# Two attention layers on one core: one quad's exps given to GpSimd as powers of 2, and the sums' copies put ahead of a small load

## The chip, the cores and the metric

The kernel runs on one core of one Trainium2 chip. The metric is the device time of one execution in microseconds (us), as the median of the runs shown; an execution that is profiled has a time of its own, given beside its span. The engines are TensorE (PE, with its weight loads PEld), VectorE (DVE), ScalarE (ACT), GpSimd (POOL) and SyncE (SP, here a DMA queue only).

## The reference, cut to what matters

```
x: [2048, 512]; A: 32 heads of 16, one shared key and value (MQA); B: 32 heads of 16, a key and value each
A: q = x @ wq, k = x @ wk, v = x @ wv
B: q, k, v = x @ wqkv
each: p = softmax(q @ k.T * 16 ** -0.5) over 2048 keys;  o = p @ v;  o @ wo
g = sigmoid((x * gate_w).sum(-1));  out = g * A + (1 - g) * B
```

So there are 64 heads with 2048 x 2048 scores each: 268 million exps. The kernel takes no maximum off before the exp; the row sums come out of the value product through columns of ones beside the values.

## The kernel before

**Work.** The scores are made transposed, keys on the partitions, in units of 128 x 1024 scores (64 keys for each of two blocks of 512 queries, two heads). Two units make a quad (the list `quads`), 32 quads a phase, and 32 phases the kernel: 2048 units in all. Phases go by four: a group is eight heads of layer a or b (the groups alternate a, b), in two halves of the queries and four heads at a time. PE makes a unit's scores (L751) in one of four PSUM tiles, `slot0` to `slot3`; an engine turns them into probabilities in one of 16 SBUF tiles (`prob`, `vec`); PE multiplies these with the values (L836) into the slot that collects the phase, and behind the phase's last quad VectorE copies that slot out (L904). `normalised` then sends the sums to DRAM and back in another layout (`held`, `each`, `back`), takes their reciprocals, and moves the products to where the output product needs them. The output products (`o_unit`), the projections of queries, keys and values (`project`) and their splitting into two f16 halves fill the gaps.

**Who makes the exps.** ScalarE makes most units with one ACTIVATE each (L782). VectorE makes the rest, whole quads taken from a phase's end (`vector_job`, `chain`): for layer a seven instructions a unit, the first from PSUM (L1003), two on the bits in SBUF (L1007, L1011) and four of a polynomial (L1016); for layer b three (L1036, L1039, L1043). Before the change GpSimd makes none: it sets a few tiles and issues DMAs.

**Order.** All of it is written out by a planner in Python while the program is built. It keeps a clock for each engine (`plan.pe`, `plan.act`, `plan.dve`, `plan.pool`, `plan.sp`), adds a fixed cost for each instruction, and at every step lets PE take the next job that the clocks allow:

```
EXP, EXP_ENDS, EXP_AFTER = 916, 1148, 456
ISSUE, ISSUE_SP, LANDS, SUM_LANDS = 480, 600, 3200, 6500
a = plan.vec(convert, 1130, 1, t + TO_VEC, (), spared)
```

What it decides is then fixed: each engine runs its list in that order, waiting by semaphores for what another engine has not finished. A tile that a DMA still reads is given back to the list of free tiles at a planned time (`returns`, `put_back`, `returned`).

Of the kernel before, what the change touches and what calls it, by code (L numbers as in the profile page):

```python
# [12 lines left out]
F32 = mybir.dt.float32  # L13
# [3 lines left out]
ALU = mybir.AluOpType  # L17
# [27 lines left out]

EXP, EXP_ENDS, EXP_AFTER = 916, 1148, 456
SCORES, HALF, PRODUCT = 215, 430, 215
SLACK, TIGHT, URGENT, SOON, AHEAD = 404, 404, 300, 500, 900
BLOCK, READ, SPACED = 256, 3400, 1500
TO_VEC, FROM_VEC, CHAINED = 255, 150, 130  # L50
X_JOB = 560
# [120 lines left out]
def _fast(ctx, tc, x, wq_a, wk_a, wv_a, wo_a, wqkv_b, wo_b, gate_w, out, flag):  # L172
# [98 lines left out]
        return later  # L271

    warm = cst.tile([P, 1], F32, name="warm")
    index = cst.tile([P, P], F16, name="index")
    level = cst.tile([P, P], F16, name="level")
    nc.vector.memset(kA[:, :BLK], 0.0)
# [121 lines left out]
    def hold():  # L398
        pair[1] = min(slots, key=slot_at)
        free["spare"] = busy[id(pair[1])] = math.inf  # L400
# [35 lines left out]
    def starts_in(m):  # L436

        return plan.act + 2 * max(m - at[0], 0) * EXP * 0.93
# [18 lines left out]
    def reads():  # L457

        for m, fn in list(waiting):
            if at[0] >= m and not (half_vec and half_vec[0] // 2 < m):  # L460
                waiting.remove((m, fn))
                fn(plan.pe)

# [166 lines left out]
    def normalised(n, half, q, raw, turned, now):  # L630

        src, gi = groups[n]
        ends = n + 1 == len(groups) and half and q
        o, d = turned[:, 0], turned[:, 1]
        queues = (nc.sync, nc.scalar, nc.gpsimd) if ends else (nc.sync,)
        if src == "a":
            moves = [(part, slice(k, P + k - 1, 2), 0, ROWS) for k, part in ((1, d), (0, o))]
        else:
            moves = [(d, DH, 0, 2), (d, 5 * DH, 2, 2), (o, 0, 0, 1), (o, 3 * DH, 1, 2), (o, 7 * DH, 3, 1)]
            moves = [(part, slice(at, at + n * DH), to * DH, n * DH) for part, at, to, n in moves]  # L640
        moves = [(*move, e) for t in (d, o) for e in range(2) for move in moves if move[0] is t and (ends or t is o)]
        if not ends:
            each = ops.tile([P, 2 * DH], F32, tag="each", name=f"each{n}{half}{q}", bufs=1)
            held, back = (dram.tile([2 * 4, BLK], F32, tag=tag, name=f"{tag}{n}{half}{q}", bufs=2) for tag in ("held", "back"))
            heads = [(slice(1, P, 2 * DH), 4)] if src == "a" else [(slice(DH, P, ROWS), 2), (slice(2 * DH, P, ROWS), 2)]
            to = 0
            for which, count in heads:
                nc.sync.dma_start(held.rearrange("(e h) q -> h e q", e=2)[to : to + count], raw[which])
                to += count
            nc.sync.dma_start(each, held.rearrange("h (c j) -> (h c) j", c=DH))  # L650
        for m, (part, at, to, n_rows, e) in enumerate(moves):
            queues[m % len(queues)].dma_start(part[ROWS * e + to :][:n_rows], raw[at, e])
        plan.sp = max(plan.sp, now) + (len(moves) + 3) * ISSUE_SP
        returns.append((plan.sp + LANDS, raw))
        o16 = ops.tile([P, 2, BLK], F16, tag="o16", name=f"o16{n}{half}{q}", bufs=8)
        o16s[n, half, q] = o16
        cut = P if ends else BLK // 2

        def over(c):
            nc.vector.reciprocal(d[:, c : c + cut], d[:, c : c + cut])  # L660

        def gated():
            nc.vector.reciprocal(each, each)
            nc.vector.scalar_tensor_tensor(each, each, UP, gate_in[:, "ab".index(src), half], op0=ALU.mult, op1=ALU.mult)

        def spread(end):
            def moved():
                nc.sync.dma_start(back.rearrange("h (c j) -> (h c) j", c=DH), each)
                for e in range(2):
                    for h in range(4):  # L670
                        at = h if src == "a" else h % 2 * 2 + h // 2
                        nc.sync.dma_start(d[ROWS * e + h * DH :][:DH], back[4 * e + at : 4 * e + at + 1].to_broadcast([DH, BLK]))

            begun[0] = plan.on_sp([moved], end, 9 * ISSUE_SP) + 2 * LANDS

        def times(c):
            if ends:
                nc.vector.scalar_tensor_tensor(o[:, c : c + cut], o[:, c : c + cut], UP, d[:, c : c + cut], op0=ALU.mult, op1=ALU.mult)
            else:
                nc.vector.tensor_tensor(o[:, c : c + cut], o[:, c : c + cut], d[:, c : c + cut], op=ALU.mult)  # L680

        def high(c):
            (nc.scalar.copy if ends else nc.vector.tensor_copy)(o16[:, 0, c : c + cut], o[:, c : c + cut])  # L683

        def low(c):
            nc.vector.tensor_sub(o16[:, 1, c : c + cut], o[:, c : c + cut], o16[:, 0, c : c + cut])

        if ends:
            tail.append((over, times, high, low))
            return  # L690
        due = now + (30000 if n + 1 < len(groups) else 6000)
        begun = [math.inf]

        def then(end):
            ready["o16", n, half, q] = end + FROM_VEC
            put_back(end + FROM_VEC, turned)

        def spreads(end):
            spread(end)
            for c in range(0, BLK, cut):  # L700
                b = plan.vec(lambda c=c: times(c), 330, 3.4, begun[0], (), None, due)
                e = plan.vec(lambda c=c: high(c), 200, 3.3, 0.0, (b,), None, due)
                plan.vec(lambda c=c: low(c), 330, 3.2, 0.0, (e,), then if c else None, due)

        plan.vec(gated, 430, 3.5, now + 7500, (), spreads, due,
                 room=lambda: ready.get("gates", math.inf) <= plan.dve)
# [5 lines left out]
    probs, pending, vector = {}, {ph: [] for ph in range(len(phases))}, set()  # L712
    free_tiles, owed, returns = deque(tile for tile in prob_tiles if tile is not prob_tiles[-2]), [0], []
    at, part, pv_at, put_in = [0], [0], [0], [0]
    half_vec, chains = [], {}
    wrote = {"n": 0, "seen": 0}
    borrowed = {}
    filled, since = deque(), {}
# [1 line left out]
    def put_back(t, *tiles):  # L720
        for tile in tiles:
            since[id(tile)] = t
            free_tiles.append(tile)

    def spare_tiles():
        return max(len(free_tiles) - owed[0] - len(filled), 0)
# [5 lines left out]
    def laid(ph, c, p):  # L732
        n, half, q = phases[ph]
        src, gi = groups[n]
        t = ready.get(("q", src, gi, half, p), math.inf)
        if src == "b":
            t = max(t, ready.get(("k", "b", gi, c // 8, p), math.inf))
        return t

    def products(u, bank):  # L740
        m, e = divmod(u, 2)
        ph, c, w = quads[m]
        n, half, q = phases[ph]
        src, gi = groups[n]
        p = q + e
        k = kA if src == "a" else K[gi, p]
        for hh in range(2):
            for a in range(0, P, COLS):
                key = c * P + (a + ROWS * w) % P
                j = a // ROWS  # L750
                nc.tensor.matmul(bank[a : a + COLS, hh], k[rows(hh), key : key + COLS],  # L751
                                 Q[src, gi, half, p][rows(hh), j * BLK : (j + 1) * BLK], start=True, stop=True)
# [179 lines left out]
    def pick(now):  # L932
# [15 lines left out]
            return None  # L948
        return 2 * found[-1]

    def pressing():

        if not half_vec:
            return False
        ph = quads[half_vec[0] // 2][0]
        return ph <= quads[min(at[0], len(quads) - 1)][0] and left_in(ph) * EXP < CHAIN
# [116 lines left out]
    def spare_job(now):  # L1073

        if current:
            return current[0].jobs[0]
        if free["spare"] > now or min(slot_at(slot) for slot in slots) > now:
            return None
        if put_in[0] >= QUADS - 2 and put_in[0] + len(pending[pv_at[0]]) >= QUADS:
            return None  # L1080
        if half_vec:
            job = vector_job(now)
            if job or pressing():
                return job
        able = [u for u in units if u.can(now)]
        if not hurry(now):
            job = vector_job(now)
            if job:
                return job
        if not able:  # L1090
            return None
        unit = min(able, key=lambda u: u.due())
        if spare_tiles() < BEGIN and not hurry(now) and len(unit.jobs) > 8 and at[0] < 32 * LASTS:
            return None
        units.remove(unit)
        unit.begin()
        current.append(unit)
        hold()
        return unit.jobs[0]
# [195 lines left out]
    def returned():  # L1295

        for back in list(returns):
            if back[0] <= plan.pe:
                returns.remove(back)
                put_back(back[0], back[1])  # L1300

    def past(m):
        return lambda: at[0] >= m
# [399 lines left out]
```

## Time and profile before

| | |
|---|---|
| two timed runs | 1767.23 and 1771.4 us, median 1769.32 us |
| profiled execution | 1778.6 us, its span 1776.7 us |
| PE busy | 1721.5 us (97%) |
| PEld busy | 994.1 us (56%) |
| VectorE busy | 1310.5 us (74%) |
| ScalarE busy | 1706.3 us (96%), 1840 exps among it |
| GpSimd busy | 192.2 us (11%), nearly all of it DMA issue |

A row of a group names the line, the engine, the operation, the tiles (written <- read), the shapes and the count, then busy us and mean ns. A row of waits names who waited for what: us in all, times, longest. A row of a line's own view gives the shortest, median and longest duration in ns, and when the first and the last began. A row of the timeline gives start and duration in us. Instructions of one engine overlap a little, so durations add up to more than the pace.

### The profile page before, as it was taken

Reading aid. Unit: us, or ns where it says so; the run is one execution under the profiler, and the core shown is the slowest. Engines: PE = TensorE matmul, PEld = TensorE weight load, DVE = VectorE, ACT = ScalarE, POOL = GpSimd, SP = SyncE. Lnnn points to the kernel's source line nnn. Section 1 sums busy time; section 2 is a strip of 40 time slices with the busy share of each in tenths; the row PEclk is TensorE's granted clock in tenths of the full one; section 3 lists DMA queues with packets and bytes.
Section 4 is the critical chain, followed back from the end, with each engine's and each line's share of the span. In section 5 each row is a group of like instructions: output and inputs, shape, how many; then the busy total and the mean of one; then the engine's idle time right before and its main releaser. Section 6 shows DMA issues by size and latency. Waiting matters only on the chain. (4 is left out here: it accounts for less than half of the span.)

```text
span 1776.7 us, 109255 instructions
## 1 busy us (share of the span) xinstructions
PE 1721.5 (97%) x51099; PEld 994.1 (56%) x51099; DVE 1310.5 (74%) x1503; ACT 1706.3 (96%) x1856; POOL 192.2 (11%) x314
## 2 busy tenths in 40 slices
PE   8999999999999999999999999999999999999996
PEld 5555655555555565555655566555555555545453
DVE  5467689986758784996774976699586787499944
ACT  5999999999999999999999999999999999999994
POOL 1101000000000111001111121000211221100000
PEclk9999999999999999999999999999999999999998
DMA  4212110113122222112223222111322322111321
GB/s 144 68 44 61 46 41 22 40 35 72 38 55 52 53 67 61 31 37 51 45 52 64 45 66 54 50 28 40 65 39 53 58 59 70 28 46 29 105 64 63
DMA packets 71152, 95.12 MB, mean 54 GB/s; under 512 B 27580, under 2 KB 36060, under 8 KB 70692
## 3 DMA queue, kind: packets, MB, share of 16 engines
q1 hardware_dynamic: 53892, 58.61, 12.4%
q0 software_dynamic: 13568, 27.22, 7.8%
q8 instruction: 402, 6.59, 1.6%
q10 hardware_dynamic: 3232, 2.23, 0.4%
q14 instruction: 58, 0.48, 0.1%
HBM read 23.45 MB, written 17.81 MB: 23 GB/s over the span
## 5 line engine op out<-in xcount | busy, mean ns | idle before, releaser
L782 ACT ACTIVATE prob<-slot 128x1024 f32<-128x1024 f32 x1121 | 1115.9, 1101 | 15.7 <-PE slot L751 9.1
L782 ACT ACTIVATE vec<-slot 128x1024 f32<-128x1024 f32 x707 | 734.8, 1104 | 11.4 <-PE slot L751 7.5
L836 PE MATMUL slot<-prob,vA 64*32 64x256 f32 (+1 forms) x7816 | 510.5, 443 | 0.8 <-issue 0.5
L836 PE MATMUL slot<-prob,vB 64*32 64x256 f32 (+1 forms) x7464 | 502.8, 446 | 1.2 <-issue 1.1
L751 PE MATMUL slot<-Qa,kA 64*32 64x512 f16 x8192 | 442.5, 379 | 7.4 <-DVE xT L328 2.5
L751 PE MATMUL slot<-Qb,K 64*32 64x512 f16 x8192 | 411.2, 380 | 25.8 <-ACT prob L782 12.3
L836 PE MATMUL slot<-vec,vB 64*32 64x256 f32 (+1 forms) x4792 | 381.8, 454 | 0.4 <-issue 0.3
L836 PE MATMUL slot<-vec,vA 64*32 64x256 f32 (+1 forms) x4456 | 358.6, 446 | 0.1
L751 PEld LDWEIGHTS <-K 64*32 64x32 f16 x8192 | 189.6, 90 | 276.1 <-issue 216.6
L751 PEld LDWEIGHTS <-kA 64*32 64x32 f16 x8192 | 196.3, 90 | 240.6 <-issue 175.3
L836 PEld LDWEIGHTS slot<-prob,vA 64*32 64x32 f32 x7816 | 206.6, 106 | 46.5 <-issue 9.5
L836 PEld LDWEIGHTS slot<-prob,vB 64*32 64x32 f32 x7464 | 199.4, 106 | 48.8 <-issue 14.4
L836 PEld LDWEIGHTS slot<-vec,vB 64*32 64x32 f32 x4792 | 139.8, 106 | 28.7 <-issue 7.5
L836 PEld LDWEIGHTS slot<-vec,vA 64*32 64x32 f32 x4456 | 135.9, 106 | 25.9 <-issue 4.2
L1036 DVE TENSOR_SCALAR prob<-slot 128x1024 f32<-128x1024 f32 x94 | 114.6, 1219 | 17.6 <-PE slot L751 10.2
L1016 DVE SCALAR_TENSOR_TENSOR prob<-prob,prob 128x1024 f32<-128x1024 f32 x69 | 84.0, 1219 | 0.6
L1016 DVE SCALAR_TENSOR_TENSOR prob<-prob,vec 128x1024 f32<-128x1024 f32 x63 | 76.7, 1219 | 0.5
L215 PEld LDWEIGHTS <-o 64*32 64x32 f16 x3072 | 54.3, 93 | 35.8 <-ACT o L683 7.4
L1003 DVE TENSOR_SCALAR prob<-slot 128x1024 int32<-128x1024 f32 x44 | 53.8, 1222 | 26.6 <-PE slot L751 19.1
L904 DVE COPY prob<-slot 128x1024 f32<-128x1024 f32 x18 | 22.0, 1221 | 68.4 <-PE slot L836 44.7
L215 PE MATMUL slot<-w16ob,o 64*32 64x512 f16 x1536 | 63.9, 390 | 7.3 <-ACT o L683 5.7
L1036 DVE TENSOR_SCALAR vec<-slot 128x1024 f32<-128x1024 f32 x48 | 58.5, 1220 | 13.2 <-PE slot L751 10.3
(187 smaller groups left out, 1700.9 us busy)
## 6 DMA issues: line engine op xcount, KB each, us to landing
vB<-vB SPq DMA_DIRECT2D x32, 192.0 KB
out_dram<-prob POOLq DMA_DIRECT2D x44, 128.0 KB, 4.0
prob<-back SPq DMA_DIRECT2D x160, 32.0 KB
xT<-out_dram SPq DMA_DIRECT2D x16, 256.0 KB
out_dram<-xT SPq DMA_DIRECT2D x12, 256.0 KB
vec<-back SPq DMA_DIRECT2D x88, 32.0 KB
vec<-in_A_x_dram SPq DMA_DIRECT2D x10, 256.0 KB
out_dram<-prob SPq DMA_DIRECT2D x20, 128.0 KB
```

What stands on the lines that cost most here:

```text
L215: nc.tensor.matmul(outs[n : n + COLS, i], lhs[i][rows(i), n : n + COLS], rhs[i][rows(i)], start=start, stop=stop)
L751: nc.tensor.matmul(bank[a : a + COLS, hh], k[rows(hh), key : key + COLS], Q[src, gi, half, p][rows(hh), j * BLK : (j + 1) * BLK], start=Tr ...
L782: nc.scalar.activation(probs[u], sc, AF.Exp, scale=SCALE / (UP * UP))
L836: nc.tensor.matmul(pair[0][32 * k : 32 * k + 32, i, cols], v[rows(i)], probs[2 * m + k // 2][rows(i), hh, cols], start=first, stop=last)
L904: nc.vector.tensor_copy(state["raw"], full)
L1003: nc.vector.tensor_scalar(tile("p").bitcast(I32), pair[1], SCALE / (UP * UP) / math.log(2) * 2.0 ** 23, None, op0=ALU.mult)
L1016: nc.vector.scalar_tensor_tensor(p, m if i == 3 else p, VEC[i], m if i else w, op0=ALU.add, op1=ALU.mult)
L1036: nc.vector.tensor_scalar(tile("p"), pair[1], CUBE[0] * SCALE / (UP * UP), CUBE[1], op0=ALU.mult, op1=ALU.add)
```

## The change

A quad may now be given to GpSimd (`pool_job`). PE makes the unit's scores as for a chain, VectorE scales them from PSUM into an SBUF tile (one instruction, new L992), and GpSimd replaces each quarter of the tile (128 x 256) by 2 to that power, in place (four instructions, new L996). The planner gives a quarter 12000 ns and allows two such quads; its conditions come together once, for one quad of phase 9 (layer a): two units, eight pieces. The quad's value product is planned behind its last piece. In the same edit `normalised` issues the load of `each` behind the copies of the products instead of ahead of them, the tile that those copies read is given back 3000 ns later in the plan, and a transfer of queries or keys also waits for a half-made GpSimd quad. All other moves follow from the planner's clocks. In the order of instructions ScalarE has 1844 exps (1840 before), VectorE 64 chains of layer a and 138 of layer b (66 and 142).

```diff
+SLACK, TIGHT, URGENT, SOON, AHEAD, LATER = 404, 404, 300, 500, 900, 3000
+POWER, MOST = 12000, 2
...
+    two = cst.tile([P, 1], F32, name="two")
+    nc.vector.memset(two, 2.0)
...
-            if at[0] >= m and not (half_vec and half_vec[0] // 2 < m):
+            if at[0] >= m and not any(u // 2 < m for u in half_vec + half_pool):
...
-            nc.sync.dma_start(each, held.rearrange("h (c j) -> (h c) j", c=DH))
         for m, (part, at, to, n_rows, e) in enumerate(moves):
             queues[m % len(queues)].dma_start(part[ROWS * e + to :][:n_rows], raw[at, e])
+        if not ends:
+            nc.sync.dma_start(each, held.rearrange("h (c j) -> (h c) j", c=DH))
...
+    def pool_pick(now):
+        if half_pool:
+            return half_pool[0]
+        ph = quads[min(at[0], len(quads) - 1)][0] + 1
+        if at[0] < 32 or ph > LASTS or starts_in(32 * ph + 32) < now + 8 * POWER + 12000:
+            return None
...
+    def pool_job(now):
+        if plan.pool > now + 1500 or plan.backlog(2) > 2500 or powers[0] >= MOST:
+            return None
...
+            def scaled():
+                nc.vector.tensor_scalar(tile, pair[1], SCALE / (UP * UP) / math.log(2), None, op0=ALU.mult)
+            def power(i, c):
+                part = tile[:, i, c : c + BLK // 2]
+                nc.gpsimd.tensor_tensor(part, two.to_broadcast([P, BLK // 2]), part, op=ALU.pow)
+            def then(end):
+                release(end + FROM_VEC)
+                fns = [lambda i=i, c=c: power(i, c) for i in range(ACT) for c in (0, BLK // 2)]
+                done = plan.on_pool(fns, end, POWER)
+                probs[u] = tile
+                chains[m] = max(chains.get(m, 0), done + 500)
+                if e:
+                    pending[quads[m][0]].append((m, chains[m]))
+            plan.vec(scaled, 1130, 1, plan.pe + SCORES + TO_VEC, (), then)
...
+        job = pool_job(now)
+        if job:
+            return job
...
-                put_back(back[0], back[1])
+                put_back(back[0] + LATER, back[1])
```

GpSimd's list before, where the second transfer of a layer-a query block (`Qa_11847` and following, phases 10 and 11) follows the first:

```order
L422 DMA Qa_9651<-hiqa_9618 32x1024
L422 DMA Qa_9651<-loqa_9619 32x1024
L422 DMA Qa_11847<-hiqa_11818 32x1024
L422 DMA Qa_11847<-loqa_11819 32x1024
L422 DMA Qa_11848<-hiqa_11818 32x1024
```

GpSimd's list now, at the same place (ISA is a call that comes with the power instruction):

```order
L425 DMA Qa_9653<-loqa_9621 32x1024
L996 ISA
L996 TENSOR_TENSOR vec_108<-two,vec_108 128x256 x4
L425 DMA Qa_11847<-hiqa_11826 32x1024
L425 DMA Qa_11847<-loqa_11827 32x1024
L425 DMA Qa_11848<-hiqa_11826 32x1024
L425 DMA Qa_11848<-loqa_11827 32x1024
L425 DMA Qa_11849<-hiqa_11826 32x1024
L425 DMA Qa_11849<-loqa_11827 32x1024
L425 DMA Qa_11850<-hiqa_11826 32x1024
L425 DMA Qa_11850<-loqa_11827 32x1024
L996 TENSOR_TENSOR prob_103<-two,prob_103 128x256 x4
```

Four pieces stand ahead of those eight DMAs and four behind them; the first four have nothing between them, nor have the last.

VectorE's list before, at the start of phase 8 (L599 takes an output product out of PSUM, L1003 to L1016 are a chain of layer a, L904 copies the phase's product out):

```order
L599 TENSOR_SCALAR prob_103<-slot_79 128x1024
L1003 TENSOR_SCALAR prob_104<-slot_81 128x1024
L1007 TENSOR_SCALAR prob_99<-prob_104 128x1024
L1011 TENSOR_SCALAR prob_98<-prob_104 128x1024
L1016 SCALAR_TENSOR_TENSOR prob_104<-prob_99 128x1024
L904 COPY vec_107<-slot_80 128x1024
```

The same place now (L992 is the scaling of the first unit; a chain's lines are L1065, L1069, L1073 and L1078, the copy's L908):

```order
L602 TENSOR_SCALAR vec_107<-slot_79 128x1024
L992 TENSOR_SCALAR vec_108<-slot_81 128x1024
L908 COPY prob_100<-slot_80 128x1024
L1065 TENSOR_SCALAR prob_101<-slot_81 128x1024
L1069 TENSOR_SCALAR prob_102<-prob_101 128x1024
L1073 TENSOR_SCALAR vec_110<-prob_101 128x1024
L1065 TENSOR_SCALAR prob_103<-slot_82 128x1024
L1078 SCALAR_TENSOR_TENSOR prob_101<-prob_102 128x1024
```

The scaling has come in ahead of the copy, and a quad's two chains follow it, the second of which takes `slot_82` out of PSUM behind the bit instructions of the first.

VectorE's list now at the second unit, one phase later (L602 takes out an output product that PE makes in `slot_79` behind the scaling):

```order
L908 COPY prob_99<-slot_79 128x1024
L1078 SCALAR_TENSOR_TENSOR prob_97<-prob_97,prob_101 128x1024
L992 TENSOR_SCALAR prob_103<-slot_79 128x1024
L1078 SCALAR_TENSOR_TENSOR prob_102<-prob_102,prob_104 128x1024 x2
L1078 SCALAR_TENSOR_TENSOR prob_102<-prob_102,prob_105 128x1024
L602 TENSOR_SCALAR prob_104<-slot_79 128x1024
```

Three instructions with two inputs in SBUF stand between the scaling and the next one that empties a slot for PE. Before there was no such scaling here.

More of the change, by code (lines that the diff above doesn't have):

```diff
@@ L47 @@
 SCORES, HALF, PRODUCT = 215, 430, 215
-SLACK, TIGHT, URGENT, SOON, AHEAD = 404, 404, 300, 500, 900
+SLACK, TIGHT, URGENT, SOON, AHEAD, LATER = 404, 404, 300, 500, 900, 3000
+POWER, MOST = 12000, 2
 BLOCK, READ, SPACED = 256, 3400, 1500
@@ L714, in _fast @@
     at, part, pv_at, put_in = [0], [0], [0], [0]
-    half_vec, chains = [], {}
+    half_vec, half_pool, chains = [], [], {}
     wrote = {"n": 0, "seen": 0}
@@ L949, in pick, with job @@
         return 2 * found[-1]
+    def pool_pick(now):
[4 more added lines that the diff above has]
+            return None
+        found = [m for m in range(32 * ph, 32 * ph + 32) if m not in vector]
+        if not found or max(laid(ph, NT - 1, phases[ph][2] + e) for e in range(2)) + 3000 > now:
+            return None
+        return 2 * found[-1]
+    def pool_job(now):
+        if plan.pool > now + 1500 or plan.backlog(2) > 2500 or powers[0] >= MOST:
+            return None
+        u = pool_pick(now)
+        if u is None or spare_tiles() < (1 if half_pool else KEPT):
+            return None
+        def job():
+            m, e = divmod(u, 2)
+            vector.add(m)
+            while at[0] in vector:
+                at[0] += 1
+            if e:
+                half_pool.clear()
+                powers[0] += 1
+            else:
+                half_pool.append(u + 1)
+            plan.takes(16)
+            hold()
+            products(u, pair[1])
+            tile = pick_tile()
+            def scaled():
[9 more added lines that the diff above has]
+                chains[m] = max(chains.get(m, 0), done + 500)
+                if e:
+                    pending[quads[m][0]].append((m, chains[m]))
+            plan.vec(scaled, 1130, 1, plan.pe + SCORES + TO_VEC, (), then)
+        return job, SCORES
+    powers = [0]
     def pressing():
```

## The prediction

> **What bounds the kernel now.** I read the page's first part, then the groups, then ScalarE's own waits.
>
> ```profile
> span 1776.7 us, 109255 instructions
> PE 1721.5 (97%) x51099; PEld 994.1 (56%) x51099; DVE 1310.5 (74%) x1503; ACT 1706.3 (96%) x1856; POOL 192.2 (11%) x314
> L782 ACT ACTIVATE prob<-slot 128x1024 f32<-128x1024 f32 x1121 | 1115.9, 1101 | 15.7 <-PE slot L751 9.1
> L782 ACT ACTIVATE vec<-slot 128x1024 f32<-128x1024 f32 x707 | 734.8, 1104 | 11.4 <-PE slot L751 7.5
> ```
>
> ScalarE and PE are both full. Which one sets the pace shows in the stretch in which all the exps run (a window on L782; columns: us, busy with count, clock, DMA share, GB/s) and in ScalarE's waits:
>
> ```profile
> 24.60:1752.00 1727.40, 1696.31 (x1840) 1.00 0.21 51
> ACT prob L782 <- PE slot L751: 9.1, 15, 1.9
> ACT vec L782 <- PE slot L751: 7.5, 17, 1.3
> ACT prob L782 <- DMA prob<-prob: 4.1, 3, 2.1
> ACT vec L782 <- DMA vec<-vec: 1.4, 1, 1.4
> ```
>
> 1840 exps in 1727.40 us are 0.939 us each, with under 30 us of idle time in all; the 1101 ns of one overlaps its neighbour's. ScalarE sets the pace, and PE follows it closely. So an exp taken away or added is worth about 0.94 us, and whatever holds PE's list up for longer than the two or three scored units ahead of ScalarE holds up the end by the same time: nothing later can make it good.
>
> **What ScalarE itself gains and loses.** The two units given to GpSimd do not leave ScalarE with less: its list has 1844 exps instead of 1840, because the planner now makes six chains fewer on VectorE. That is 4 x 0.94 = **3.8 us more**. In return the moved load and the later return of tiles aim at ScalarE's waits for a DMA that still reads the tile, 4.1 + 1.4 = 5.5 us above. The load waits on SP for the sums' trip through DRAM:
>
> ```profile
> SPq L650 <- DMA held<-prob: 23.4, 20, 1.5
> DVE each L663 <- DMA each<-held: 6.3, 3, 3.7
> ```
>
> Up to 1.5 us (23.4 / 20 = 1.2 us) stand in SP's queue ahead of the copies (L652) each time. With the copies first they read their tile that much sooner; the load goes later by the issue of two or six copies, and behind it wait the reciprocal on VectorE (6.3 us of waits already, three times) and the spreading DMAs, which the planner starts 30 us ahead of need. Between nothing and 5.5 us regained, I take half: **-2.8 us**. The swap in widths of the value products (352 fewer of 256 columns, 176 more of 512) and the six chains fewer lighten engines that are not the bound: nothing, as ScalarE's own pace covers it. Were that cover gone, a chain of layer a is worth some 7.5 us of VectorE.
>
> **What GpSimd's work does to VectorE.** Before the change GpSimd computes nothing, but at one place it writes SBUF for a while beside a VectorE instruction of the kind that the chains use. First GpSimd's timeline and the view of its line, then VectorE's timeline, then the view of line L1007 and its neighbour L1016:
>
> ```profile
> 135.79 1.86 POOL L1338 MEMSET vB<- 128x1024 f32 x2
> L1338 POOL MEMSET vB<- x2: 971/972/972, 135.8 to 136.7; 128x1024 f32 x2
> 136.24 1.95 DVE L1007 TENSOR_SCALAR prob<-vec 128x1024 int32<-128x1024 int32 x1
> 138.12 1.21 DVE L1003 TENSOR_SCALAR prob<-slot 128x1024 int32<-128x1024 f32 x1
> L1007 DVE TENSOR_SCALAR prob<-vec x17: 684/686/1954, 116.4 to 1479.1; 128x1024 int32<-128x1024 int32 x17
> L1016 DVE SCALAR_TENSOR_TENSOR prob<-prob,prob x69: 1206/1218/1227, 228.7 to 1520.9; 128x1024 f32<-128x1024 f32 x69
> ```
>
> An L1007 takes 686 ns; this one took 1954 ns. It began at 136.24 inside the first memset, the second ended at 135.79 + 1.86 = 137.65, and the instruction ended at 136.24 + 1.95 = 138.19, so 0.54 us behind the second. It waited for **both** memsets: the gap between two GpSimd instructions did not let it in. I read this as an exclusive hold on something both engines need, for as long as GpSimd's instructions follow each other. L1016, with two inputs in SBUF, was never longer than 1227 ns, but no L1016 ran beside a memset.
>
> Now a piece's length. No row of before shows the power instruction. From below there is half a memset's price, 972 / 4 = 0.24 us; from above the 12 us that the changed plan reserves, stretched as its other constants are short of their rows (916 against 939 ns for an exp, 480 against 540 for this issue, 1130 against 1219 for this instruction), at most by 540 / 480, to 13.5 us:
>
> ```profile
> L422 POOL DMA_DIRECT2D Qb<-loqb x32 | 17.3, 540 | 5.8 <-DVE loqb L490 5.1 <-DMA each<-held 0.7
> L1036 DVE TENSOR_SCALAR prob<-slot 128x1024 f32<-128x1024 f32 x94 | 114.6, 1219 | 17.6 <-PE slot L751 10.2 <-ACT prob L782 3.7 <-ACT vec L782 3.5
> L1007 DVE TENSOR_SCALAR prob<-prob 128x1024 int32<-128x1024 int32 x23 | 16.0, 696 | 0.7
> L1011 DVE TENSOR_SCALAR prob<-prob 128x1024 int32<-128x1024 int32 x23 | 15.7, 686 | 0.0
> ```
>
> The ends lie far apart; the plan's other constants come within 15% of rows, so I take 12 us, 48 us for a unit's four.
>
> **First unit.** Behind its scaling (1.3 us with the wait for it) GpSimd starts. VectorE copies the product out and takes the first chain's scores from PSUM, then comes to the bit instructions, the kind that stood still above, and stands until the fourth piece is done. The second chain's scores are queued behind them, so `slot_82` stays full, and PE's list comes to its next use of that slot after twelve more units scored for ScalarE. ScalarE works on for 12 x 0.94 = 11.3 us; then it starves until 1.3 + 48 + 0.69 + 0.69 + 1.22 = 51.9 us have passed. Loss: 51.9 - 11.3 = **40.6 us**.
>
> **Second unit.** Behind its scaling stand three L1078 (two inputs in SBUF, 1.22 us each) and then the L602 that empties the output product; PE needs that slot after nine ScalarE units, 8.5 us. If L1078 stands too, the loss is 1.3 + 48 + 4 x 1.22 - 8.5 = 45.7 us. If only the bit instructions stand, VectorE goes on to the next chain's L1069 and PE starves after 17 units: 1.3 + 48 + 2 x 0.69 + 3 x 1.22 - 17 x 0.94 = 38.4 us. The trace shows no L1016 beside GpSimd's work, so both are open; the kind that is shown is the second, and a power instruction reads as well as writes, which a memset does not. I take the first, **45.7 us**, and keep 38.4 for the range.
>
> The Trainium skill ("SBUF — State Buffer", "Who interferes with whom") says that a VectorE instruction with two SBUF inputs contends with a GpSimd instruction that reads SBUF and not with one that only writes it, and that the loser blocks for the whole of the other's instruction. By it the second unit costs 45.7 us; by the L1007 row alone it costs 38.4 us. No row here can show which, since the memsets read nothing.
>
> The eight DMAs of GpSimd between the two groups of pieces, and its DMAs behind the last, stand in a gap of its queue that is wide before the change:
>
> ```profile
> 405.54 0.54 POOL L422 DMA_DIRECT2D Qa<-loqa  x1
> 486.06 0.54 POOL L422 DMA_DIRECT2D Qa<-hiqa  x1 [79.98 <-DVE hiqa L487]
> 491.11 0.54 POOL L422 DMA_DIRECT2D Qa<-loqa  x1
> 584.42 1.26 POOL L220 DMA_DIRECT2D w16qb<-w16qb  x2 [92.78 <-PE slot L751]
> ```
>
> 80 us and 93 us idle hold 48 us each, so those DMAs cost nothing. VectorE is behind when released, and is busy 40.17 of 50 us here, so it catches up a little slowly; PE next needs it some 14 us on, for about 16 us of its work. I put nothing for that and leave it to the range.
>
> ```profile
> 425.00:475.00 50.00, 49.89 (x1512) 28.44 (x1503) 40.17 (x43) 49.77 (x55) 0.00 (x0) 1.00 0.22 50
> ```
>
> **The sum.** 40.6 + 45.7 + 3.8 - 2.8 = 87.3 us on the profiled execution's 1778.6 us: 1865.9. That execution was 9.3 us above the median of the runs shown (1769.32), so the forecast is 1856.6, rounded to **1857 us**. With pieces of 8 us it would be 32 us less, with 13.5 us 12 us more: its own range is 1818 to 1876.
>
> **The rivals.**
> - *GpSimd works beside VectorE* (not slower). A memset writes without a pause, a power computes 47 ns for each of its 256 columns, and may hold what it shares only in moments. Then VectorE loses nothing; ScalarE has 3.8 us more and 2.8 us less, 1769.3 + 1.0 = **1770 us** (1764 to 1778). For it: twelve us for 256 columns is a hundred times a memset's pace, 972 / 4 = 243 ns. Against it: the L1007 row, which waited through a gap between two instructions. It decides from a hold of about 10 us a unit down, since PE has that cover.
> - *The hold is short*: VectorE gets in between pieces and finds several microseconds, or a piece is nearer 5 us. Then 8 x 5 = 40 us less 20 us of cover and some service: **1795 us** (1785 to 1812), on both sides of the 2% line at 1804.7.
> - *PE waits for the last piece.* Without a hold, 57 exps (53.5 us) lie between the second scaling and the value product of that quad, which needs 1.3 + 48 us: 4 us to spare, so it decides from a piece of 13 us. At 16 us it costs 12 us: **1782 us**.
> - *The change is not what it says*: two quads were allowed and one is made. That is in the sum already; it halves what the hold costs and adds no rival time.
>
> **How the numbers follow.** Forecast 0.54, no hold 0.34, short hold 0.08, late piece 0.04. About 2% (35 us) is what a measurement of this kernel can tell from no change. Slower by over 2%: 0.54 + 0.04 of the short hold, 0.58; the rest of the rivals within 2%, 0.40, and 0.02 for faster, which would need 38 exps gone. As signs are so split, the range runs from the no-hold case to the forecast's upper end: 1766 to 1876.
>
> **What would show it.** In the profile after: a L1069 or L1078 of tens of microseconds beside GpSimd's L996, between about 420 and 540 us; ScalarE idle some 40 us twice there, with PE waiting for VectorE at L755; a mean of L996 near 12 us; 1844 exps; the rest of the timeline at its old pace; the waits for `prob<-prob` DMAs nearly gone. L1078 at 1.22 us beside L996 would put the forecast wrong at its root; a mean of L996 far from 12 us would put its size wrong.

## The result: slower by 12.7%, and the profile after

The median after the change is **1995.65 us** (1995.28 and 1996.03), 1.1272 times the time before in the same runs (95% interval 1.1248 to 1.1296). The profiled execution took 1995.28 us with a span of 1993.4 us, 216.7 us more than the span before. The forecast was 1857 us, its range 1766 to 1876: the sign was right, the size and the mechanism were not.

First the page of the profile after, its totals, its slices (one is 49.8 us), and its groups of exps and of powers:

```profile
span 1993.4 us, 108547 instructions
PE 1723.6 (86%) x50747; PEld 975.4 (49%) x50747; DVE 1286.9 (65%) x1480; ACT 1709.5 (86%) x1860; POOL 522.2 (26%) x322
DVE  6377799867703100524995867749977767859943
ACT  5999999999803100999999999999999999999994
POOL 1110000007999999111003112110012021110000
PEclk9999999999956655999999999999999999999998
L786 ACT ACTIVATE prob<-slot 128x1024 f32<-128x1024 f32 x1156 | 1150.5, 1114 | 107.3 <-PE slot L755 105.6
L786 ACT ACTIVATE vec<-slot 128x1024 f32<-128x1024 f32 x676 | 709.4, 1113 | 133.8 <-PE slot L755 132.9
L996 POOL TENSOR_TENSOR vec<-two,vec 128x256 f32<-128x256 f32 x4 | 165.4, 41356 | 56.3 <-DVE vec L992 56.3
L996 POOL TENSOR_TENSOR prob<-two,prob 128x256 f32<-128x256 f32 x4 | 164.4, 41118 | 0.0
```

PE and ScalarE work as long as before, in a longer span. GpSimd is full for seven slices, and beside them ScalarE's row falls to 0, comes back to 3 and falls to 1 and 0: two holes. A piece of the power took **41.1 us**, not 12. ScalarE's waits on scores, 9.1 + 7.5 us before, are 105.6 + 132.9 us now, which is 221.9 us more; the exps' waits on DMAs, 5.5 us before, are gone. 221.9 - 5.5 = 216.4 us, about the 216.7 us between the spans. The match is partly luck: four more exps (3.8 us) and a profiled execution before that ran 9.3 us above its median are in that difference too. Beside `e1_mult` below, which has the same list, it comes out cleanly. Who holds PE up in turn is in the chain of waits (who waits <- for whom: us, times, longest), and when is in GpSimd's timeline:

```profile
PE slot L840 <- POOL prob L996: 134.4, 3, 81.1
PE slot L755 <- DMA Qa<-hiqa: 89.4, 2, 86.9
```

```profile
459.56 165.36 POOL L996 TENSOR_TENSOR vec<-two,vec 128x256 f32<-128x256 f32 x4 [56.33 <-DVE vec L992]
624.88 0.72 POOL L425 DMA_DIRECT2D Qa<-hiqa  x1
...
628.87 0.55 POOL L425 DMA_DIRECT2D Qa<-loqa  x1
629.43 164.42 POOL L996 TENSOR_TENSOR prob<-two,prob 128x256 f32<-128x256 f32 x4
```

It is one chain on GpSimd without a gap: four pieces, eight query transfers, four pieces, from 459.56 to 793.85 us. The transfers stand in GpSimd's list behind the first pieces. PE needs those queries for the scores of the next phases from about 541 us and gets them after 624.88 (89.4 us of waits); then it needs the quad's probabilities and gets the last at 793.85 (134.4 us). 89.4 + 134.4 = 223.8 us.

VectorE, which the forecast had standing still, does not. From its timeline beside the first piece, and from the view of the two-input line over the whole execution (shortest/median/longest ns):

```profile
465.94 0.69 DVE L1069 TENSOR_SCALAR prob<-prob 128x1024 int32<-128x1024 int32 x1
470.31 1.22 DVE L1078 SCALAR_TENSOR_TENSOR prob<-prob,prob 128x1024 f32<-128x1024 f32 x1
...
L1078 DVE SCALAR_TENSOR_TENSOR prob<-prob,prob x73: 1210/1222/1229, 140.2 to 1737.8; 128x1024 f32<-128x1024 f32 x73
```

0.69 and 1.22 us are what these lines took before, with GpSimd idle; the longest of the 73 is 1.229 us.

### The profile page after: what moved, and what is told of

It reads as the page before. It is cut to its first block, busy times and chain, and to the rows that moved or that the text cites. A ratio compares the mean times of both kernels' runs of the same rounds, so it can differ in the third digit from the quotient of the medians.

```text
span 1993.4 us, 108547 instructions
## 1 busy us (share of the span) xinstructions
PE 1723.6 (86%) x50747; PEld 975.4 (49%) x50747; DVE 1286.9 (65%) x1480; ACT 1709.5 (86%) x1860; POOL 522.2 (26%) x322
## 3 DMA queue, kind: packets, MB, share of 16 engines
q1 hardware_dynamic: 53892, 58.61, 10.9%
## 4 chain that ended last, share of the span: by engine, by line
PE 48%; issue 15%; ACT 14%; POOL 13%; DVE 8%; DMA 2%; SPq 0%; ACTq 0%; DVEq 0%; POOLq 0%
PE slot L840 24%; PE slot L755 14%; PE slot L216 9%; ACT prob L786 8%; POOL prob L996 8%; ACT vec L786 5%; POOL vec L996 4%; DVE prob L1098 1%; DVE prob L1101 1%; DVE prob L1105 1%; DVE vec L1098 1%; DVE vec L1105 1%; DVE vec L1101 0%; PE slot L312 0%; DVE prob L1078 0%
## 5 line engine op out<-in xcount | busy, mean ns | idle before, releaser
L786 ACT ACTIVATE prob<-slot 128x1024 f32<-128x1024 f32 x1156 | 1150.5, 1114 | 107.3 <-PE slot L755 105.6
L786 ACT ACTIVATE vec<-slot 128x1024 f32<-128x1024 f32 x676 | 709.4, 1113 | 133.8 <-PE slot L755 132.9
L840 PE MATMUL slot<-prob,vA 64*32 64x256 f32 (+1 forms) x7488 | 509.5, 453 | 134.4 <-POOL prob L996 134.4
L755 PE MATMUL slot<-Qa,kA 64*32 64x512 f16 x8192 | 437.0, 381 | 92.6 <-DMA Qa<-hiqa 89.4
L840 PE MATMUL slot<-prob,vB 64*32 64x256 f32 (+1 forms) x7680 | 511.9, 452 | 0.0
L840 PE MATMUL slot<-vec,vA 64*32 64x256 f32 (+1 forms) x4480 | 365.8, 455 | 0.5 <-issue 0.3
L840 PE MATMUL slot<-vec,vB 64*32 64x256 f32 (+1 forms) x4528 | 357.1, 444 | 0.1
L840 PEld LDWEIGHTS slot<-prob,vA 64*32 64x32 f32 x7488 | 198.9, 106 | 181.7 <-POOL prob L996 136.6
L996 POOL TENSOR_TENSOR vec<-two,vec 128x256 f32<-128x256 f32 x4 | 165.4, 41356 | 56.3 <-DVE vec L992 56.3
L996 POOL TENSOR_TENSOR prob<-two,prob 128x256 f32<-128x256 f32 x4 | 164.4, 41118 | 0.0
L908 DVE COPY prob<-slot 128x1024 f32<-128x1024 f32 x20 | 24.5, 1223 | 179.1 <-PE slot L840 157.9
L1065 DVE TENSOR_SCALAR prob<-slot 128x1024 int32<-128x1024 f32 x41 | 50.1, 1222 | 109.9 <-PE slot L755 103.8
L1098 DVE TENSOR_SCALAR prob<-slot 128x1024 f32<-128x1024 f32 x86 | 105.3, 1225 | 11.7 <-PE slot L755 5.9
L1078 DVE SCALAR_TENSOR_TENSOR prob<-prob,prob 128x1024 f32<-128x1024 f32 x73 | 89.0, 1222 | 0.7
L425 POOL DMA_DIRECT2D K<-hikb x32 | 17.5, 547 | 222.0 <-DVE hikb L490 222.0
```

The source lines that it names most:

```text
L425: fns.append(lambda q=queues[len(fns) % len(queues)], dst=dst, src=src: q.dma_start(dst, src))
L786: nc.scalar.activation(probs[u], sc, AF.Exp, scale=SCALE / (UP * UP))
L840: nc.tensor.matmul(pair[0][32 * k : 32 * k + 32, i, cols], v[rows(i)], probs[2 * m + k // 2][rows(i), hh, cols], start=first, stop=last)
L908: nc.vector.tensor_copy(state["raw"], full)
L996: nc.gpsimd.tensor_tensor(part, two.to_broadcast([P, BLK // 2]), part, op=ALU.pow)
L1065: nc.vector.tensor_scalar(tile("p").bitcast(I32), pair[1], SCALE / (UP * UP) / math.log(2) * 2.0 ** 23, None, op0=ALU.mult)
```

## The experiments

The theory after the result: **the chain of eight 41-us pieces on GpSimd's queue is the whole loss**, through what waits behind a piece. The rivals: GpSimd's work takes something from VectorE; or the rest of the change (order, later return, moved load) costs part of it. All edits but one are made to the changed kernel.

### The same pieces without the power, and no pieces at all

`e1_mult` keeps every instruction and makes each piece a multiplication. `e2_no_power` allows no such quad, so the planner writes its order anew.

```diff
-                nc.gpsimd.tensor_tensor(part, two.to_broadcast([P, BLK // 2]), part, op=ALU.pow)
+                nc.gpsimd.tensor_tensor(part, two.to_broadcast([P, BLK // 2]), part, op=ALU.mult)
```

> This kernel leaves the power out: GpSimd's eight pieces multiply by 2 instead, in the same places of the same lists, so the quad's probabilities are not exps. Theory A (the loss is the length of the power alone, 41.1 us a piece where the plan has 12): the two waits on GpSimd (89.4 us for the DMAs behind the first four pieces, 134.4 us for the last pieces) go, and the time is that of before give or take the 4 exps and the sums' move, 1764 to 1776 us. Theory B (the new order itself costs something, as a wait that the length hides): 1785 us or more, with a wait other than GpSimd's in ScalarE's list.

```diff
-POWER, MOST = 12000, 2
+POWER, MOST = 12000, 0
```

> No quad goes to GpSimd; the sums' copies ahead of the load, and the later return of their tiles, stay. Theory A: these two take away most of the 5.5 us that ScalarE waits for DMAs reading a tile, so 1763 to 1769 us, 0 to 0.35% faster than before. Rival: the plan only shifts, and the waits come back elsewhere (the load of each is later, and VectorE's reciprocals wait for it): 1769 to 1776 us.

`e1_mult`: **1767.68 us** against 1772.25 for the kernel before on that chip, 0.9978 (0.9963 to 0.9994). `e2_no_power`: 1768.9 us, 0.9984 (0.9969 to 0.9999). The view of the pieces and ScalarE's waits in `e1_mult`:

```profile
L996 POOL TENSOR_TENSOR vec<-two,vec x4: 617/617/617, 461.2 to 462.9; 128x256 f32<-128x256 f32 x4
L996 POOL TENSOR_TENSOR prob<-two,prob x4: 608/1550/1592, 518.5 to 523.1; 128x256 f32<-128x256 f32 x4
ACT prob L786 <- PE slot L755: 7.9, 15, 1.8
ACT vec L786 <- PE slot L755: 3.0, 10, 0.6
```

With pieces of 0.6 to 1.6 us in the same places, in the same order, nothing of the loss is left. (The first unit's take 0.617 us; most of the second unit's take 1.55 us, beside VectorE's three instructions with two inputs.) ScalarE's waits on scores are 7.9 + 3.0 = 10.9 us here and 238.5 us in the changed kernel, 227.6 us apart; the spans, 1766.2 and 1993.4 us, are 227.2 us apart. So the loss goes with the power in the pieces, and the rest of the change costs nothing; by these intervals it gains 0.2%. Whether it is the pieces' length or something else about the power is for the next runs.

### The transfers taken out from between the pieces

`e3_on_sp` issues those query transfers of layer a on SP's queue.

```diff
-                fns = lay(hilo, to[p], p, parts, (nc.sync, nc.gpsimd))
+                fns = lay(hilo, to[p], p, parts, (nc.sync, nc.sync) if name == "qa11" else (nc.sync, nc.gpsimd))
```

> The eight query DMAs that stand between GpSimd's two groups of pieces are issued by SP instead; all else is as in the changed kernel. Theory A (one cause: GpSimd's pieces run one after the other, and the end waits for the eighth): the first wait of some 87 us at the scores goes, but the last pieces still start only when the first four are done, so the wait at the value product grows by the same time: 1985 to 1996 us. Rival (two waits, each with its own price): about 1995 - 87 = 1909 us.

It took **1992.64 us**, 1.1243 (1.1206 to 1.1279). Its timeline of GpSimd and its chain of waits:

```profile
461.46 165.87 POOL L996 TENSOR_TENSOR vec<-two,vec 128x256 f32<-128x256 f32 x4 [56.56 <-DVE vec L992]
627.31 164.36 POOL L996 TENSOR_TENSOR prob<-two,prob 128x256 f32<-128x256 f32 x4
PE slot L840 <- POOL prob L996: 201.4, 3, 81.1
PE slot L840 <- POOL vec L996: 17.5, 1, 17.5
```

The long wait for the queries is gone (2.5 us of 89.4 are left), and the wait for the probabilities has grown to 201.4 + 17.5 = 218.9 us. The total is 3 us less, near the price of the eight issues (629.43 - 624.88 = 4.5 us). So the two holes were not two losses: either way the end of the eighth piece sets the time, and the transfers only chose where PE stood.

### One unit's power at a time

`e6_first_unit` keeps the power in the first unit and multiplies in the second, `e7_second_unit` the other way round.

```diff
-                nc.gpsimd.tensor_tensor(part, two.to_broadcast([P, BLK // 2]), part, op=ALU.pow)
+                nc.gpsimd.tensor_tensor(part, two.to_broadcast([P, BLK // 2]), part, op=ALU.mult if e else ALU.pow)
```

> The first unit's four pieces are powers, the second unit's are multiplications, which leaves the second unit's exps out. Theory A (pieces run in a row, and PE waits for what stands behind them): only the wait for the query DMAs behind the first four is left, 87 us at the scores, on the 1768 us of the kernel with multiplications alone: 1853 to 1858 us. Rival (each piece costs the end 29 us, what the plan is short of): half of the changed kernel's loss, 1880 us.

The line of `e7_second_unit` ends in `ALU.pow if e else ALU.mult`.

> The second unit's four pieces are powers, the first unit's are multiplications, which leaves the first unit's exps out. Theory A: the pieces start behind the second scaling, about 517 us, and end 164 us later, at 681; the quad's product comes at about 572 us when nothing has waited before, so 109 us of waiting, at the value product alone: 1874 to 1880 us, more than the first unit costs, though the two together cost less than their sum. Rival (half of the loss each): 1880 us for this one and for the first; or, if the power held VectorE up, bit instructions of tens of microseconds.

`e6_first_unit`: **1856.87 us** (1.0475, 1.0425 to 1.0526). `e7_second_unit`: **1884.66 us** (1.0632, 1.0583 to 1.0681), some 5 us over the upper end of what was expected. The wait of PE in the first, then the wait and the pieces' view in the second:

```profile
PE slot L755 <- DMA Qa<-hiqa: 86.8, 1, 86.8
```

```profile
PE slot L840 <- POOL prob L996: 113.6, 2, 74.4
L996 POOL TENSOR_TENSOR prob<-two,prob x4: 41115/41118/42086, 519.1 to 643.3; 128x256 f32<-128x256 f32 x4
```

With the first unit's power alone only the transfers are late: 1856.87 - 1767.68 = 89.2 us over `e1_mult` (on another chip, where the kernel before took 1770.81 us instead of 1772.25), beside one wait of 86.8 us. With the second's alone only the probabilities are late: 117.0 us over `e1_mult`, beside waits of 113.6 us. In `e7_second_unit` the last piece ends at 643.3 + 41.1 = 684.4 us; less the 113.6 us, the quad is wanted at **about 571 us**. In the changed kernel it is ready at 793.85: 223 us late, and PE's two waits there were 223.8 us.

The expectation also said that the two together cost less than their sum. They cost more: 1995.65 - 1767.68 = 228.0 us against 89.2 + 117.0 = 206.2 us. In `e7_second_unit` the powers start at 519.1 us, and in `e6_first_unit` PE works until about 541 us, so the 22 us between serve as cover in both runs; in the changed kernel, with one chain, they cover only once.

### A piece by itself

`e5_sizes` goes into the kernel before: at phase 5, three powers of 16, 32 and 64 columns and three multiplications, on a tile set to 1.0 that no result uses.

```diff
+        if ph == 5:
+            probe = index.bitcast(F32)
+            nc.gpsimd.memset(probe, 1.0)
+            for n in (16, 32, 64):
+                nc.gpsimd.tensor_tensor(probe[:, :n], two.to_broadcast([P, n]), probe[:, :n], op=ALU.pow)
+            for n in (16, 32, 64):
+                nc.gpsimd.tensor_tensor(probe[:, :n], two.to_broadcast([P, n]), probe[:, :n], op=ALU.mult)
```

> The kernel before, with six GpSimd instructions more in a gap of its queue, on a scratch tile that nobody reads: the power, then the multiplication, of 128x16, 128x32 and 128x64, all on ones. Theory A (the power costs a fixed time per column, 41.1 us / 256 = 161 ns): 2.6, 5.1 and 10.3 us, on ones as on the scores, and the multiplications under 0.4 us. Rival (most of a piece is a fixed cost, or hangs on the data): the three are nearly alike, or far from 161 ns a column. The time stays that of before.

The time, one run of 1769.07 us against 1770.81, shows no loss. The views of its two lines:

```profile
L1342 POOL TENSOR_TENSOR index<-two,index x3: 3887/5791/11307, 266.2 to 276.1; 128x16 f32<-128x16 f32 x1, 128x32 f32<-128x32 f32 x1, 128x64 f32<-128x64 f32 x1
L1344 POOL TENSOR_TENSOR index<-two,index x3: 212/239/293, 287.4 to 288.1; 128x16 f32<-128x16 f32 x1, 128x32 f32<-128x32 f32 x1, 128x64 f32<-128x64 f32 x1
```

The powers took 3.9, 5.8 and 11.3 us, each 0.7 to 1.3 us over what was expected. From 32 to 64 columns the power adds 5.5 us, 0.17 us a column, on other data and at another place; 41.1 / 256 is 0.16. A straight line through the three gives 0.157 us a column and 1.1 us besides, and by it 41 us for 256 columns. So 41 us is the price of the instruction by size, not something that its neighbours did to it. The changed kernel's own view in two windows says the same: of the first unit's pieces the first two stand beside a busy VectorE, the last two beside one that is nearly idle.

```profile
L996 POOL TENSOR_TENSOR vec<-two,vec x2: 41183/41600/42017, 459.6 to 500.7; 128x256 f32<-128x256 f32 x2
L996 POOL TENSOR_TENSOR vec<-two,vec x2: 41112/41112/41113, 542.7 to 583.8; 128x256 f32<-128x256 f32 x2
```

A busy VectorE costs a piece 0.07 and 0.90 us.

### Does GpSimd hold VectorE at all?

`e4_stream` makes each piece sixteen multiplications by 1.0 (read and write, no power, so the quad's exps are left out), `e10_memsets` thirty-two memsets (write only, exps left out too). Both keep GpSimd busy for 50 to 70 us a unit, near what the plan assumed.

```diff
-    nc.vector.memset(two, 2.0)
+    nc.vector.memset(two, 1.0)
...
-                nc.gpsimd.tensor_tensor(part, two.to_broadcast([P, BLK // 2]), part, op=ALU.pow)
+                for _ in range(16):
+                    nc.gpsimd.tensor_tensor(part, two.to_broadcast([P, BLK // 2]), part, op=ALU.mult)
```

> This kernel leaves the power out: each piece is sixteen multiplications by 1, so GpSimd streams SBUF in and out for some tens of microseconds a unit beside VectorE's chains, and the quad's probabilities are not exps. Theory A (GpSimd holds nothing of VectorE's for longer than it moves data, and the power moves data seldom): the bit instructions (0.69 us) and the instructions with two SBUF inputs (1.22 us) that begin beside these multiplications become several times longer, as L1007 did beside the memsets, and ScalarE starves for up to the length of the stream less 10 us of cover, a unit: 1790 to 1850 us. Rival (only a write without a read, as a memset's, holds VectorE up): their durations stay, and the time is that of the kernel with one multiplication a piece, about 1770 us.

```diff
-                nc.gpsimd.tensor_tensor(part, two.to_broadcast([P, BLK // 2]), part, op=ALU.pow)
+                for _ in range(32):
+                    nc.gpsimd.memset(part, 1.0)
```

> This kernel leaves out the GpSimd quad's exps: each piece is 32 memsets of 128x256 to 1, 128 in a row behind each scaling, some 0.25 to 0.3 us each, so 32 to 38 us of writing a unit with nothing between. It repeats at length the row on which the prediction rested. Theory A (one instruction in turn, as with the multiplications): bit instructions beside the memsets last 0.69 us plus at most one or two memsets, under 1.3 us, instructions with two inputs keep 1.22 us, and the time is within 10 us of the 1768 us of the kernel with multiplications alone. Rival, as the prediction read it (GpSimd keeps VectorE out until its row of instructions ends): the first bit instruction beside each row lasts 25 us or more, and the time is 1790 us or more.

`e4_stream`: **1801.45 us** (1.0164, 1.0131 to 1.0197), 33.8 us over `e1_mult`. `e10_memsets`: **1771.48 us** (0.9976, 0.9952 to 1.0001), no loss. Pieces' views and VectorE's timeline, `e4_stream` first, then `e10_memsets` (in both, L1070 is the bit instruction and L1079 the one with two inputs):

```profile
L997 POOL TENSOR_TENSOR vec<-two,vec x64: 612/841/1702, 460.2 to 525.0; 128x256 f32<-128x256 f32 x64
470.79 1.10 DVE L1070 TENSOR_SCALAR prob<-prob 128x1024 int32<-128x1024 int32 x1
471.81 1.63 DVE L1079 SCALAR_TENSOR_TENSOR prob<-prob,prob 128x1024 f32<-128x1024 f32 x1
```

```profile
462.07 51.83 POOL L997 MEMSET vec<- 128x256 f32 x128 [56.42 <-DVE vec L992]
472.23 0.78 DVE L1070 TENSOR_SCALAR prob<-prob 128x1024 int32<-128x1024 int32 x1
472.93 1.21 DVE L1079 SCALAR_TENSOR_TENSOR prob<-prob,prob 128x1024 f32<-128x1024 f32 x1
136.28 1.86 POOL L1404 MEMSET vB<- 128x1024 f32 x2
136.74 1.95 DVE L1070 TENSOR_SCALAR prob<-prob 128x1024 int32<-128x1024 int32 x1
```

Beside a row of multiplications most of the chains' instructions that read SBUF get about 0.4 us longer, none over 0.45 (L1066, which reads PSUM, keeps its 1.22 us), and GpSimd's own take 0.84 us in the median instead of 0.61, 1.70 us at the longest. That fits two engines that take turns, each waiting for at most about one instruction of the other; no row shows the turns themselves. The expectation had the time right (1790 to 1850 us) and the lengthening wrong: 1.3 to 1.6 times, not several times. Beside a row of memsets the bit instructions get up to 0.2 us longer and the others no longer. Neither row of instructions holds VectorE for its whole length. The row that the forecast was built on is in this trace too (the last two lines): the same instruction beside two long memsets takes 1.95 us again, and why that one waits for both is **open**.

The Trainium skill ("SBUF — State Buffer", "Who interferes with whom") names the pair right: two inputs in SBUF contend with a GpSimd instruction that reads (1.63 us), not with one that only writes (1.21 us). That the loser blocks for the whole of the other's instruction does not hold here for the power, beside whose 41 us the same line took 1.22 us. What the power does within those 41 us no run shows.

What such turns cost is in the windows of the exps' line (us, ScalarE busy with count, clock, DMA share, GB/s), `e1_mult` first, then `e4_stream` with one wait of PE:

```profile
455.00:535.00 80.00, 80.00 (x89) 1.00 0.20 50
535.00:620.00 85.00, 84.41 (x93) 1.00 0.22 56
```

```profile
455.00:535.00 80.00, 69.77 (x76) 0.96 0.17 41
535.00:620.00 85.00, 64.56 (x69) 0.90 0.17 42
PE slot L840 <- POOL prob L997: 10.0, 1, 10.0
```

182 exps against 145: 37 exps at 0.94 us are 34.8 us, the whole loss of `e4_stream`, in the two stretches in which GpSimd works. Not all of it is VectorE's delay: the last line, from PE's waits in `e4_stream`, is 10.0 us at the quad's value product, where PE waits for the last of GpSimd's multiplications. That is the late piece again, on a small scale.

### The rest of the change

`e8_order_only` allows no GpSimd quad and takes the 3000 ns off, so only the load's place is left. `e9_later_only` allows none and puts the load back ahead of the copies, so only the later return is left.

```diff
-SLACK, TIGHT, URGENT, SOON, AHEAD, LATER = 404, 404, 300, 500, 900, 3000
-POWER, MOST = 12000, 2
+SLACK, TIGHT, URGENT, SOON, AHEAD, LATER = 404, 404, 300, 500, 900, 0
+POWER, MOST = 12000, 0
```

> No quad for GpSimd, no later return: only the sums' copies ahead of the load of each. Theory A (the copies' earlier reading of the tile is what frees ScalarE): 0.1 to 0.3% faster than before, with ScalarE's waits for DMAs gone. Rival (the later return in the plan does it): no difference from before, and the waits still there.

```diff
-POWER, MOST = 12000, 2
+POWER, MOST = 12000, 0
...
+            nc.sync.dma_start(each, held.rearrange("h (c j) -> (h c) j", c=DH))
         for m, (part, at, to, n_rows, e) in enumerate(moves):
             queues[m % len(queues)].dma_start(part[ROWS * e + to :][:n_rows], raw[at, e])
-        if not ends:
-            nc.sync.dma_start(each, held.rearrange("h (c j) -> (h c) j", c=DH))
```

> No quad for GpSimd, the load of each ahead of the copies as before: only the tiles' later return in the plan (3000 ns). Theory A: the planner no longer hands out a tile that a DMA still reads, so ScalarE's waits for DMAs go here too, but it has one tile less for 3 us at each phase; no difference from before within 0.2%. Rival (the return alone is the gain): 0.15 to 0.3% faster.

`e8_order_only`: 1771.02 us against 1774.06 on its chip, 0.9979 (0.9969 to 0.999). `e9_later_only`: 1769.68 us, 0.9977 (0.9967 to 0.9988). With both edits (`e2_no_power`) it was 0.9984. VectorE's wait for the load, `e8_order_only` first, then `e9_later_only`:

```profile
DVE each L667 <- DMA each<-held: 18.8, 9, 5.7
```

```profile
DVE each L666 <- DMA each<-held: 6.3, 2, 3.8
```

Each edit alone gains about 0.2%, and together no more. For the copies' order that is what theory A expected; for the later return the rival came out. The exps' waits for a DMA that still reads the tile are gone from all three traces, which fits two edits that serve the same end. But those waits are no sure price. In `e5_sizes`, whose lists are those of the kernel before but for a few small instructions on GpSimd and VectorE, they are these:

```profile
ACT prob L784 <- DMA prob<-prob: 0.7, 1, 0.7
ACT prob L784 <- DMA vec<-prob: 0.4, 1, 0.4
```

That is 1.1 us where the profiled execution of before had 5.5, so what the 0.2% comes from is open. Moving the load makes VectorE wait 18.8 us instead of 6.3, which costs nothing that these times show. The kernels without the power are the ones that beat both before and after; the 0.2% is all there is, and which of them is best these intervals do not tell.

## Why the prediction was wrong, step by step

- **What bounds the kernel: right.** ScalarE sets the pace, and what holds PE's list beyond its cover is lost at the end in full: 37 exps not made were 34 us in `e4_stream`, and 227.6 us more of ScalarE's waits on scores than in `e1_mult` were 227.2 us of span.
- **The step "Now a piece's length ... I take 12 us" failed first.** No row of before showed the power, and the upper end, 13.5 us, was the plan's own constant stretched by 540 / 480. That the plan's other constants lie within 15% of rows says nothing of an operation that the plan had no row for. It measured 41.1 us, 3.4 times as much. An instruction without a row had a lower bound and no upper one, and the range should have said so.
- **The step "an exclusive hold ... for as long as GpSimd's instructions follow each other" failed too**, independently of the size: VectorE's lines beside the pieces kept 0.69 and 1.22 us, and in `e4_stream` and `e10_memsets` they got at most 0.45 us longer where the step had a hold for the whole row. It rested on one odd row. The test that the prediction set itself, "L1078 at 1.22 us beside L996 would put the forecast wrong at its root", came out that way. The right piece would not have saved it: with 41.1 us the two holds become 1.3 + 164.4 + 2.6 - 11.3 = 157.0 and 1.3 + 164.4 + 4.9 - 8.5 = 162.1 us, 319 us together, where 217 to 228 were measured.
- **"80 us and 93 us idle hold 48 us each, so those DMAs cost nothing" fell with the 12 us.** 165 us do not fit into 80, and the transfers that were to be free held PE for 89.4 us. The gap was read rightly; the thing put into it was not.
- **The rival "PE waits for the last piece" had the mechanism**, at a chance of 0.04. Its own sum with the measured piece is 1.3 + 4 x 41.1 - 53.5 = 112.2 us for the second unit alone; `e7_second_unit` waited 113.6. For both units: the changed kernel's trace has 118 exps (111 us) between the start of the first piece, 459.56 us, and PE's stop at the quad's value product, about 657 us, so 8 x 41.1 + 4.5 - 111 = 222 us, against 216.7 in spans over the kernel before and 227.2 over `e1_mult`. On that path the rival gave the first unit's pieces no part, since at 12 us they would have been done. To be hidden, the eight would have had to be (111 - 4.5) / 8 = 13.3 us each at most.
- **"+3.8 us" and "-2.8 us".** The count was right (1844 exps). Together the terms made +1.0 us; with short pieces the same list measured -4.6 us (`e1_mult`, 0.22% with an interval of 0.06 to 0.37%). Of the 5.5 us of DMA waits, taken by half, 1.2 us are left in `e1_mult` and none in the changed kernel; but the 5.5 us were one execution's, with 1.1 us in `e5_sizes`. So neither the -2.8 us nor the measured gain is traced to these waits, and what the gain comes from is open.
- **Small things in the working.** The lower end of a piece's length, called half a memset's price, is a quarter of it (972 / 4). The upper end of the forecast's own range, 1876 us, is 7 us above what its working gives, 1857 + 12 = 1869 us.

## What to carry to other kernels

An operation that no trace shows has no upper price: run it once by itself, at two sizes, before a plan is built on it; here a straight line through three instructions of 16 to 64 columns gives 41 us for 256. On an engine that works its list in order, long pieces add up and hold everything that stands behind them, DMA issues included, so the check is the end of the last piece against the moment when its product is wanted, not the length of one piece against one gap. A single strange row is a question and no rule.

## What was not expected of the hardware

The granted TensorE clock fell while PE waited. PE's windows in the changed kernel, the two holes, the 6 us behind the second, and after (us, then busy time with count of PE, PEld, VectorE, ScalarE and GpSimd, the clock, DMA share, GB/s):

```profile
541.00:629.00 88.00, 1.27 (x24) 0.62 (x32) 0.65 (x2) 0.90 (x2) 87.99 (x11) 0.52 0.04 10
659.00:794.00 135.00, 3.08 (x44) 0.85 (x52) 0.00 (x0) 1.02 (x1) 134.85 (x4) 0.51 0.00 0
794.00:800.00 6.00, 6.00 (x140) 2.99 (x148) 4.88 (x5) 3.47 (x4) 0.00 (x0) 0.72 0.16 52
800.00:850.00 50.00, 49.61 (x1478) 27.75 (x1463) 28.18 (x37) 49.38 (x55) 6.00 (x10) 1.00 0.22 57
```

0.52 and 0.51 in the holes, a mean of 0.72 in the first 6 us of work, 1.00 from 800 us on. Beside waits of 89 and 134 us this restart is small.

In `e5_sizes` the first power also stood behind a wait of its own. A memset comes right before it, and GpSimd's timeline shows 7.39 us in between in which it waited for nothing that the trace names. What that was is open; in the changed kernel GpSimd waits 56.33 us for the scaling at that place, so such a wait would not show.

```profile
258.67 0.17 POOL L1340 MEMSET index<- 128x64 f32 x1
266.23 3.89 POOL L1342 TENSOR_TENSOR index<-two,index 128x16 f32<-128x16 f32 x1 [7.39 <-issue]
```
